# Block 2's gate stretch of a two-MLP kernel: transfers asked for four steps ahead in a held queue, the last norm's mean three steps later

## The chip, the cores and the metric

One core of a Trainium2 chip runs the whole program. The metric is the device time of one execution in microseconds (us); lower is better. The core's engines run their own instruction queues side by side and wait for each other by semaphores: TensorE (PE, matrix products; PEld is its weight load), VectorE (DVE), ScalarE (ACT), GpSimd (POOL) and SyncE (SP, whose queue here asks for nearly all transfers).

## The reference

Three stages, for 1536 tokens of width 512 (2 sequences of 768, 8 heads of 64). The weights of both MLPs and the scale of the norm are taken in double precision.

```python
state = gamma[None, :, None, None] * state + np.einsum('bhd,bhe->bhde', k[:, :, t], v[:, :, t])
y[:, :, t] = scale * np.einsum('bhd,bhde->bhe', q[:, :, t], state)
...
h = x @ w_in
g = h * (1.0 / (1.0 + np.exp(-1.702 * h)))
return (g @ w_out).astype(np.float32)
...
rms = np.sqrt(np.mean(x * x, axis=-1, keepdims=True) + 1e-06)
xn = x / rms * rms_g
g = xn @ w_gate
silu = g * (1.0 / (1.0 + np.exp(-g)))
val = xn @ w_val
return (silu * val @ w_out).astype(np.float32)
```

The first MLP is 512 to 2048 to 512, the second 512 to 1536 (gate and value) to 512.

## The kernel before

**Numbers.** Each float32 operand of a product is split into a high part (ScalarE's copy, name ending in h) and a low part (VectorE's difference, ending in l); `product` (L379) makes three matmuls of it: high by high (L383), high by low and low by high (L384, L385). A weight that comes in double precision (a tile `w_64`, `w<-in_w` in the rows) is converted by `convert` (L151): two copies on ScalarE (L163, L164), three steps on VectorE (L167, L168, L174), and for the second MLP's weights a store to DRAM (L180, `w27d<-qw`), to be read back by `reload` (L188, `w24r<-w24d`). `load_next` asks for the next double tile, `convert_next` converts one and calls `load_next`. In the trace all buffers of a pool go by one name: `w` is a double tile as well as a part of w3 (the second MLP's out-weights).

**Stages.** The 1536 tokens are three blocks of 512 columns. Attention runs for all; the first MLP has 16 slices f of 128 hidden units. Block 0 is computed in the loop over f with weights `wo`. Blocks 1 and 2 come from the chains m0 to m7 of `seven` (L692), which compute two slices for two blocks with seven products instead of eight (the steps use the operand combinations x, y, z; their banks are called a and b, the intermediate results p, q, r). Of each result, block 1's gate is used at once (`use_m`, L646: silu on ScalarE at L653, `gate_parts` at L421 and L422 splits it into gh and gl, out-weights `wowp`), and block 2's gate gm is stored to DRAM (`to_dram`). After the chains comes the **gate stretch** of block 2: for each f the gate gwm is read back, split, and multiplied by out-weights `wowq` into the banks acc. In it the norm of the earlier blocks runs on ScalarE and VectorE, and at its end the first sums of the second MLP's weights.

**The norm.** `norm_tasks` (L453) gives six tasks: two of squares sq and their sum with its split into sh and sl; the mean (two matmuls with `mean_w`, L479) with the first guess r and u (L483, L486); the `roots`; and two of scaling. There is one norm for each block; the last, of block 2, runs in the walk over the second MLP's first chains.

**The second MLP** has for each pair of slices (g = 0, 2, ...) two chains, g0, v0 and so on (gate and value), whose 14 steps are walked in turn; `work[n]` holds what is issued behind step n: the products o of earlier slices, conversions, reloads, the sums and splits of the next weights (`set_tasks`, L590: sums swg and swv at L611; operands wg2x, wg2y, wg2z and likewise wv), the norm's tasks, and `y_tasks`, the operands yo of block 2 (differences at L578, splits at L388). From the third pair on, the chains lg and lv of block 2 are walked behind each pair.

**What sets the order.** Every engine works its queue in order. A scheduler sets the order within an engine from the order in which the program is written and the times at which it takes buffers and operands to be ready; `after` (L123) adds a fixed order between two instructions, `in_order` (L104) one for all instructions of a stretch. A tile of a pool can be written only when the tile that had its buffer is no longer read, so a load waits for that. Pools here: `wr` 16 buffers, `tmp` 12, `wo` 3, `gs` 3, `st` 4. `wait_m` (L986) asks for gate and out-weights of f; it is called two steps ahead.

Of the kernel before, what the change touches and what calls it, by code (L numbers as in the profile page):

```python
# [8 lines left out]
F32 = mybir.dt.float32  # L9
# [27 lines left out]
FIRST, OTHER, LAST = 0, 1, 2  # L37
LAG = 3
JOIN = 4
HELD = 2  # L40
# [6 lines left out]
def tile_retention_mlp_swiglu(  # L47
# [56 lines left out]

    def in_order(first):

        last = {}
        for i in nc.cur_bb.bb.instructions[first:]:
            if i.engine in ENGINES:
                if i.engine in last:  # L110
                    after(i, last[i.engine])
                last[i.engine] = i
        return last
# [24 lines left out]

    def convert_next(split=False):
        n = count["converted"]  # L140
        if n < len(queue):
            rest = convert(*queue[n])
            count["converted"] += 1
            if split:
                return rest
            for step in rest:
                step()
            load_next()

# [58 lines left out]

    def load_wo(f, user):
        t = wo_p.tile([128, 1024], F32R, tag="wo", name=f"wo{user}{f}")  # L210
        parts[user, f] = both(t)
        nc.sync.dma_start(out=t.bitcast(F32), in_=kept["wo", f])
# [243 lines left out]
    def norm_tasks(j, p):  # L456
# [19 lines left out]
        def means():  # L476
            st["m"] = psum(p, f"mean{j}")
            for n, t in enumerate(st.pop("two")):
                nc.tensor.matmul(out=st["m"], lhsT=mean_w, rhs=t, start=n == 0, stop=n == 1)  # L479

        def guess():
# [167 lines left out]
    def use_m(p):  # L649
        def use(i, j, src, own):  # L650
            f = 2 * p + i
            if j == 0:
                nc.scalar.activation(out=own, in_=src, func=ACTF.Silu, scale=GELU)  # L653
                gate_parts(("wp", f), own)
                load_wo(f, "wp")
                fill.extend((f, m) for m in range(KD))
            else:
                t = later["gs"].tile([128, T], F32, tag="gs", name=f"gm{f}")
                nc.scalar.activation(out=t, in_=src, func=ACTF.Silu, scale=GELU)
                to_dram("m", f, t)  # L660
        return use
# [282 lines left out]
    assert not att  # L944

    lanes = [[(p, n) for p in range(k, F1 // 2, 2) for n in range(7)] for k in range(2)]
    chains = {
# [16 lines left out]
    for e, (p, n) in enumerate(order):  # L964
# [14 lines left out]
        if e > 12 and e % 2:  # L979
            if count["converted"] < 2 * F1 + 20:  # L980
                convert_next()
        if e in (24, 32):
            some(norm, 1)
    some(norm, 1)

    def wait_m(f):  # L986
        if f < F1:
            t = waiting["m", f] = later["gs"].tile([128, T], F32, tag="gs", name=f"gwm{f}")
            nc.sync.dma_start(out=t, in_=kept_g["m", f])
            load_wo(f, "wq")  # L990

# [9 lines left out]
    some(norm, 1)  # L1001
    wait_m(0)
    wait_m(1)
    gate_m(0)
    tasks = None
    for f in range(F1):
        wait_m(f + 2)
        gate_m(f + 1)
        some(norm, 2 if f == 0 else 1)
        if f == 0:  # L1010
# [3 lines left out]
        if f in (4, 5, 6, 8, 10, 12):  # L1014
            some(norm, 1)
        if f == 8:
            for x in range(2):
                reload("w2", x)
        if f == 10:
# [5 lines left out]
        if f == F1 - 1:  # L1025
            some(norm, len(norm))
            for n in (0, 3, 4):
                for t in sets:
                    t[n]()
        mlp1_out("wq", 2, f)  # L1030
    for m in range(KD):
        evacuate(2, m)
# [37 lines left out]
    for g in range(0, F2, 2):  # L1070
# [15 lines left out]
        if g == 0:  # L1086
            for n, t in zip((2, 4, 8, 11), norm):
                work[n].append(t)
        if g == 2:
            norm = norm[4:] + y_tasks()  # L1090
            for n, t in enumerate(norm):
                work[min(n, 13)].append(t)
# [117 lines left out]
```

## Time and profile before

| | |
|---|---|
| time, median of 3 runs | 592.88 us (592.82 to 595.37) |
| the profiled execution | 591.96 us, of which the span is 588.5 us |
| TensorE | 579.9 us busy (99%), 3264 matmuls |
| VectorE | 453.4 us busy (77%) |
| ScalarE | 363.1 us busy (62%) |
| GpSimd | 26.3 us busy (4%) |
| TensorE clock granted | 1.00 of full speed over the span |
| transfers | 135.09 MB, 230 GB/s |

The span runs from the first to the last instruction that the profiler records; the rest of the execution's time lies around it. The gate stretch lies at 260 to 309 us. A matmul's row shows 0.39 us, but the next one can start before it ends, so the space between two starts tells what one costs. TensorE's busy share hides small waits for the same reason; a wait shows as a wider space between two starts, and in the rows as the idle time in square brackets with what ended it.

### The profile page before, as it was taken

How to read it: one execution, taken by the hardware profiler on the slowest of the kernel's cores; microseconds unless marked ns; L12 is line 12 of the kernel's file. 1: busy time of each engine (PE TensorE's matmuls, PEld its weight loads, DVE VectorE, ACT ScalarE, POOL GpSimd, SP SyncE). 2: the span in 40 equal slices, each digit the busy share in tenths (PEclk: the TensorE clock that was granted, in tenths of full speed). 3: DMA queues.
4: the chain of work that ended last, by engine and by line, in shares of the span. 5: the costliest groups of instructions: out<-in, count | busy, mean ns of one | idle time of the engine just before them, and what ended most of it. 6: DMA issues, size and time to landing. Idle time of an engine off the chain costs nothing.

```text
span 588.5 us, 9253 instructions
## 1 busy us (share of the span) xinstructions
PE 579.9 (99%) x3264; PEld 480.7 (82%) x3264; DVE 453.4 (77%) x808; ACT 363.1 (62%) x688; POOL 26.3 (4%) x27
## 2 busy tenths in 40 slices
PE   8999999999999999999999999999999999999997
PEld 5787887888788888877877888888989889988885
DVE  2999897978999786649989999997765676654542
ACT  2686767766777786657457876555654445544432
POOL 4400321000000000000000000000000000000000
PEclk9999999999999999999999999999999999999999
DMA  8979989896379888888893555736323476543521
GB/s 323 400 241 404 356 301 360 288 308 249 142 240 340 296 273 311 285 302 294 301 336 121 184 150 173 235 107 215 108 71 108 122 264 227 175 144 121 167 72 71
DMA packets 47854, 135.09 MB, mean 230 GB/s; under 512 B 5568, under 2 KB 5824, under 8 KB 47808
## 3 DMA queue, kind: packets, MB, share of 16 engines
q1 hardware_dynamic: 47376, 134.37, 66.4%
q8 instruction: 25, 0.41, 0.3%
q10 hardware_dynamic: 432, 0.14, 0.1%
q14 instruction: 21, 0.17, 0.1%
HBM read 98.84 MB, written 35.65 MB: 229 GB/s over the span
## 4 chain that ended last, share of the span: by engine, by line
PE 83%; DMA 7%; DVE 5%; ACT 2%; issue 1%; SPq 0%; DVEq 0%
PE acc L383 6%; PE acc L385 6%; PE acc L384 6%; PE o L383 6%; PE o L384 6%; PE o L385 6%; PE h L406 5%; DMA w<-in_w 3%; DMA qk<-in_qk 1%; PE y L308 1%; DMA wowq<-wo11d 1%; PE m0a L711 1%; PE g4a L711 1%; DMA wm2d<-w 1%; PE sc L266 1%
## 5 line engine op out<-in xcount | busy, mean ns | idle before, releaser
L383 PE MATMUL o<-w,gh 128*128 128x512 f32 x144 | 56.2, 390 | 0.0
L384 PE MATMUL o<-w,gh 128*128 128x512 f32 x144 | 56.2, 390 | 0.0
L385 PE MATMUL o<-w,gl 128*128 128x512 f32 x144 | 56.1, 389 | 0.0
L168 DVE CUSTOM_DVE_ANT_0 qw<-qw,uw 128x1024 uint16<-128x1024 uint16 x68 | 47.3, 698 | 3.1 <-ACT uw L164 0.9
L163 ACT ACTIVATE qw<-w 128x512 f32<-128x512 f32 x68 | 45.1, 663 | 1.5 <-DMA w<-in_w 1.5
L164 ACT ACTIVATE uw<-w 128x512 uint32<-128x512 uint32 x68 | 45.3, 667 | 0.0
L167 DVE TENSOR_SCALAR qw<-qw 128x512 uint32<-128x512 uint32 x68 | 30.6, 451 | 17.2 <-ACT qw L163 17.2
L389 DVE TENSOR_TENSOR gl<-gw,gh 128x512 fp32r<-128x512 f32 x24 | 16.6, 692 | 26.1 <-ACT gh L388 26.0
L388 ACT ACTIVATE gh<-gw 128x512 fp32r<-128x512 f32 x24 | 15.1, 630 | 28.6 <-PE o L384 23.5
L385 PEld LDWEIGHTS o<-w,gl 128*128 128x128 f32 x144 | 27.0, 188 | 5.6
L384 PEld LDWEIGHTS o<-w,gh 128*128 128x128 f32 x144 | 27.1, 188 | 4.7
L383 PEld LDWEIGHTS o<-w,gh 128*128 128x128 f32 x144 | 27.1, 188 | 4.5
L383 PE MATMUL acc<-gh,wo 128*128 128x512 f32 x64 | 25.8, 411 | 0.0
L383 PE MATMUL acc<-gh,wowq 128*128 128x512 f32 x64 | 25.3, 396 | 0.5 <-DMA wowq<-wo11d 0.4
L385 PE MATMUL acc<-gh,wo 128*128 128x512 f32 x64 | 25.1, 393 | 0.0
L384 PE MATMUL acc<-gl,wo 128*128 128x512 f32 x64 | 25.1, 392 | 0.0
L384 PE MATMUL acc<-gl,wowp 128*128 128x512 f32 x64 | 25.1, 392 | 0.0
L384 PE MATMUL acc<-gl,wowq 128*128 128x512 f32 x64 | 25.0, 390 | 0.0
L385 PE MATMUL acc<-gh,wowp 128*128 128x512 f32 x64 | 24.9, 390 | 0.0
L385 PE MATMUL acc<-gh,wowq 128*128 128x512 f32 x64 | 24.9, 390 | 0.0
L174 DVE SCALAR_TENSOR_TENSOR qw<-w,qw 128x512 uint32<-128x512 uint32 x36 | 24.6, 685 | 0.2
L406 PE MATMUL h<-xt0h,wih 128*128 128x512 f32 x64 | 24.4, 397 | 0.2 <-ACT xt0h L329 0.2
(1512 smaller groups left out, 1693.4 us busy)
## 6 DMA issues: line engine op xcount, KB each, us to landing
w<-in_w SPq DMA_DIRECT2D x68, 512.0 KB, 5.9
qk<-in_qk SPq DMA_DIRECT2D x12, 512.0 KB, 7.9
kv<-in_kv SPq DMA_DIRECT2D x12, 512.0 KB, 8.3
gmd<-gm SPq DMA_DIRECT2D x16, 256.0 KB, 4.6
gwm<-gmd SPq DMA_DIRECT2D x16, 256.0 KB, 3.9
g1d<-gs SPq DMA_DIRECT2D x12, 256.0 KB, 2.5
g2d<-gl SPq DMA_DIRECT2D x12, 256.0 KB, 2.0
gw<-g1d SPq DMA_DIRECT2D x12, 256.0 KB, 2.7
```

Source lines behind the costliest of these rows:

```text
L163: nc.scalar.activation(out=q, in_=high.bitcast(F32), func=ACTF.Copy, scale=2.0 ** -112)
L164: nc.scalar.activation(out=t, in_=low, func=ACTF.Copy, scale=2.0 ** -29)
L167: lambda: nc.vector.tensor_scalar(out=m, in0=m, scalar1=3, scalar2=None, op0=ALU.logical_shift_left),
L168: lambda: nc.vector.tensor_tensor(out=m, in0=m, in1=t, op=ALU.add),
L174: nc.vector.scalar_tensor_tensor(out=dst, in0=high, scalar=0x80000000, in1=m, op0=ALU.bitwise_and, op1=ALU.bitwise_or)
L383: nc.tensor.matmul(out=out, lhsT=ah, rhs=bh, start=first, stop=False)
L384: nc.tensor.matmul(out=out, lhsT=ah, rhs=bl, start=False, stop=False)
L385: nc.tensor.matmul(out=out, lhsT=al, rhs=bh, start=False, stop=last)
L388: nc.scalar.activation(out=hi, in_=src, func=ACTF.Copy)
L389: nc.vector.tensor_tensor(out=lo, in0=src, in1=hi.bitcast(F32), op=ALU.subtract)
L406: nc.tensor.matmul(out=ps, lhsT=w[a][:, k * 128:(k + 1) * 128], rhs=x[b][:, k, :], start=o == order[0], stop=o == order[-1])
L711: nc.tensor.matmul(out=bank, lhsT=u, rhs=v, start=first and k == 0 and x == 0, stop=k == 1 and x == 2, skip_group_check=True,)
```

## The change

Five things, all in the order and the buffers; no arithmetic changes.

- `wait_m` becomes `load_wq`. The gate tile gwm comes from `tmp` (12) instead of `gs` (3), and out-weights of ten of the sixteen f from `wr` (16) instead of `wo` (3). It is called four steps ahead instead of two; the first four and the out-weights wowp15 are asked for inside the loop over the chains, at its fourth-last step.
- From there to the end of the gate stretch the transfers in SyncE's queue are held in the order of the program (`in_order`, now with a choice of engines).
- Four loads of double tiles (of w27 and w33), which the last conversions of the chain loop asked for, are asked for in steps 11 to 14 of the gate stretch; the two reloads of w2 go from step 8 to steps 6 and 8.
- A mean matmul is held behind the TensorE instruction that the program wrote last before it.
- The last norm's mean and guess go from step 8 to step 11 of the walk over g0 and v0, and its roots from step 11 to the next pair.

```diff
+AHEAD = 4
+WITH_WR = (0, 1, 2, 3, 4, 5, 6, 10, 11, 12)
...
-    def in_order(first):
+    def in_order(first, engines=ENGINES):
...
-            if i.engine in ENGINES:
+            if i.engine in engines:
...
-    def convert_next(split=False):
+    def convert_next(split=False, load=True):
...
-            load_next()
+            if load:
+                load_next()
...
-    def load_wo(f, user):
-        t = wo_p.tile([128, 1024], F32R, tag="wo", name=f"wo{user}{f}")
+    def load_wo(f, user, p=None):
+        p = p or wo_p
+        t = p.tile([128, 1024], F32R, tag=p.name, name=f"wo{user}{f}")
...
         def means():
             st["m"] = psum(p, f"mean{j}")
+            done = [i for i in nc.cur_bb.bb.instructions if i.engine == mybir.EngineType.PE][-1]
             for n, t in enumerate(st.pop("two")):
                 nc.tensor.matmul(out=st["m"], lhsT=mean_w, rhs=t, start=n == 0, stop=n == 1)
+                after(nc.cur_bb.bb.instructions[-1], done)
...
-                load_wo(f, "wp")
+                if ("wp", f) not in parts:
+                    load_wo(f, "wp")
...
+    def load_wq(f):
+        if f < F1:
+            t = waiting["m", f] = tmp(f"gwm{f}")
+            nc.sync.dma_start(out=t, in_=kept_g["m", f])
+            load_wo(f, "wq", wr_p if f in WITH_WR else wo_p)
...
-                convert_next()
+                convert_next(load=count["converted"] < 2 * F1 + 16)
         if e in (24, 32):
             some(norm, 1)
+        if e == len(order) - 4:
+            loads = len(nc.cur_bb.bb.instructions)
+            load_wo(F1 - 1, "wp")
+            for f in range(AHEAD):
+                load_wq(f)
...
-    def wait_m(f):
-        if f < F1:
-            t = waiting["m", f] = later["gs"].tile([128, T], F32, tag="gs", name=f"gwm{f}")
-            nc.sync.dma_start(out=t, in_=kept_g["m", f])
-            load_wo(f, "wq")
...
-    wait_m(0)
-    wait_m(1)
     gate_m(0)
     tasks = None
     for f in range(F1):
-        wait_m(f + 2)
+        load_wq(f + AHEAD)
         gate_m(f + 1)
+        if f > F1 - 6 and f < F1 - 1:
+            load_next()
...
-        if f == 8:
-            for x in range(2):
-                reload("w2", x)
+        if f in (6, 8):
+            reload("w2", f // 2 - 3)
...
         mlp1_out("wq", 2, f)
+    in_order(loads, [mybir.EngineType.SP])
...
         if g == 0:
-            for n, t in zip((2, 4, 8, 11), norm):
+            for n, t in zip((2, 4, 11), norm):
                 work[n].append(t)
         if g == 2:
-            norm = norm[4:] + y_tasks()
+            norm = norm[3:] + y_tasks()
```

The scheduler moves more than these lines. Three places follow, each as the engine's queue stands before and after. Lines of the kernel after are higher by 4 to 7 (L711 is now L718).

**At the end of the last chain.** TensorE, before: behind the last row of the chain's result m7b (bank b of m7) stand eight rows of slice 14 of block 1 (gate parts gl_2846 and gh_2845) and both rows of the mean of an earlier block, ahead of the products of slice 15, whose gate (gh_2910) is made from m7b.

```order
L711 MATMUL m7b<-xm_1920,wm7zl 128x512
L384 MATMUL acc_1_1875<-gl_2846,wowp_2849 128x512
L385 MATMUL acc_1_1875<-gh_2845,wowp_2849 128x512
L383 MATMUL acc_2_1876<-gh_2845,wowp_2849 128x512
L384 MATMUL acc_2_1876<-gl_2846,wowp_2849 128x512
L385 MATMUL acc_2_1876<-gh_2845,wowp_2849 128x512
L383 MATMUL acc_3_1877<-gh_2845,wowp_2849 128x512
L384 MATMUL acc_3_1877<-gl_2846,wowp_2849 128x512
L385 MATMUL acc_3_1877<-gh_2845,wowp_2849 128x512
L479 MATMUL mean_2928<-sh_2451,mean_w 128x512
L479 MATMUL mean_2928<-sl_2452,mean_w 128x512
L383 MATMUL acc_0_1874<-gh_2910,wowp_2914 128x512
```

TensorE, after, from the same row of m7b (slice 15's gate is gh_2920 here):

```order
L718 MATMUL m7b<-xm_1920,wm7zl 128x512
L484 MATMUL mean_2936<-sl_2452,mean_w 128x512
L387 MATMUL acc_0_1874<-gh_2920,wowp_2871 128x512
L387 MATMUL acc_1_1875<-gh_2920,wowp_2871 128x512
L387 MATMUL acc_2_1876<-gh_2920,wowp_2871 128x512
```

Of the ten rows one is left there; the others stand further up. ScalarE, after, at the same place (the silu is qm<-qm; before, r and u stood behind both gh):

```order
L666 ACTIVATE gm_2908<-m7a 128x512
L489 ACTIVATE r_2939<-mean_2936 128x512
L659 ACTIVATE qm_2829<-qm_2829 128x512
L492 ACTIVATE u_2940<-r_2939 128x512
L425 ACTIVATE gh_2920<-qm_2829 128x512
L425 ACTIVATE gh_2967<-gwm_2873 128x512
```

The norm's u now stands between the silu and the split of slice 15's gate.

**Where the last norm's mean stood.** TensorE, before, in the walk over g0 and v0 (o is a product of the second MLP's out-weights):

```order
L711 MATMUL g0a<-xh_3243,wg0yl 128x512
L479 MATMUL mean_3546<-sh_3489,mean_w 128x512
L383 MATMUL o_3708<-w_3712,gh_3457 128x512
L384 MATMUL o_3708<-w_3712,gh_3457 128x512
L385 MATMUL o_3708<-w_3712,gl_3458 128x512
L479 MATMUL mean_3546<-sl_3490,mean_w 128x512
L711 MATMUL v0a<-xh_3243,wv0yh 128x512
```

TensorE, after, from the same row of g0a:

```order
L718 MATMUL g0a<-xh_3243,wg0yl 128x512
L718 MATMUL v0a<-xh_3243,wv0yh 128x512
L718 MATMUL v0a<-xl_3244,wv0yh 128x512
L718 MATMUL v0a<-xh_3243,wv0yl 128x512
L718 MATMUL v0a<-xh_3243,wv0yh 128x512
```

The y products of v0a follow g0a's at once; the mean and the o products stand further down.

**At the first products of the second MLP.** VectorE, before, ahead of the addition pg<-g0b that ends the first product pair (w_3712 is a part of w30, swg and swv are sums of the weights w22 and w23):

```order
L447 COPY x_2_3394<-acc_3_2986 128x512
L611 TENSOR_TENSOR swg_3511<-swg_3511,w22r 128x256
L611 TENSOR_TENSOR swv_3520<-swv_3520,w22r 128x256
L611 TENSOR_TENSOR swg_3511<-w22r,w23r 128x256
L611 TENSOR_TENSOR swg_3511<-w22r,swg_3511 128x256
L611 TENSOR_TENSOR swv_3520<-w22r,w23r 128x256
L611 TENSOR_TENSOR swv_3520<-w22r,swv_3520 128x256
L389 TENSOR_TENSOR wg2zl<-w23r,wg2zh 128x256
L389 TENSOR_TENSOR wg2zl<-swg_3511,wg2zh 128x512
L721 TENSOR_TENSOR pg_3408<-g0b,pg_3408 128x512
```

VectorE, after, up to the same addition and past it:

```order
L451 COPY x_2_3394<-acc_1_2984 128x512
L451 COPY x_2_3394<-acc_3_2986 128x512
L393 TENSOR_TENSOR w_3710<-w30r,w_3710 128x512
L728 TENSOR_TENSOR pg_3408<-g0b,pg_3408 128x512
L170 TENSOR_SCALAR qw_3423<-qw_3423 128x512
L171 ISA qw_3423<-qw_3423,uw_3424 128x1024
```

The sums of w22 and w23 and the low parts of wg2z stand behind pg now, in the rows up to the first difference x<-x of block 2's operands. In TensorE's queue nine o products stood ahead of the first z product of g2a before; after, four do:

```order
L718 MATMUL v2a<-xh_3243,wv2yl 128x512
L387 MATMUL o_3706<-w_3815,gh_3617 128x512
L387 MATMUL o_3707<-w_3815,gh_3617 128x512
L387 MATMUL o_3708<-w_3815,gh_3617 128x512
L387 MATMUL o_3709<-w_3815,gh_3617 128x512
L718 MATMUL g2a<-xh_3269,wg2zh 128x512
```

The other o products of that slice come later.

## Rows read from the trace of the kernel before

**Rows 1.** Windows: length, busy PE, PEld, DVE, ACT, POOL, PEclk, DMA share, GB/s.

```profile
259.94:309.00 49.06, 48.50 (x209) 38.60 (x209) 45.60 (x69) 31.28 (x51) 0.00 (x0) 1.00 0.88 306
309.00:330.00 21.00, 19.59 (x86) 15.87 (x86) 20.66 (x42) 17.41 (x33) 0.00 (x0) 1.00 0.45 136
330.00:355.00 25.00, 25.00 (x112) 20.67 (x112) 25.00 (x45) 18.05 (x34) 0.00 (x0) 1.00 0.57 178
...
366.00:584.00 218.00, 218.00 (x1196) 189.75 (x1195) 140.99 (x274) 108.05 (x218) 0.00 (x0) 1.00 0.45 147
```

**Rows 2.** Timeline at m7's end: start, duration, engine, line, instruction, [idle before <-releaser].

```profile
257.44 0.39 PE L711 MATMUL m7b<-xm,wm7zl 128*128 128x512 f32 x1
...
257.87 0.69 DVE L721 TENSOR_TENSOR qm<-m7b,qm 128x512 f32<-128x512 f32 x1 [2.40 <-PE m7b L711]
...
258.60 0.63 ACT L653 ACTIVATE qm<-qm 128x512 f32<-128x512 f32 x1 [1.51 <-DVE qm L721]
...
259.94 0.96 PE L383 MATMUL acc<-gh,wowp 128*128 128x512 f32 x3
...
261.86 0.63 ACT L486 ACTIVATE u<-r 128x512 f32<-128x512 f32 x1
```

**Rows 3.** Timeline of TensorE in the gate stretch.

```profile
294.28 0.39 PE L711 MATMUL g0a<-xoh,wg0xh 128*128 128x512 f32 x1
295.07 0.50 PE L383 MATMUL acc<-gh,wowq 128*128 128x512 f32 x1 [0.41 <-DMA wowq<-wo11d]
...
308.61 0.39 PE L385 MATMUL acc<-gh,wowq 128*128 128x512 f32 x1
```

**Rows 4.** Timeline at the last norm's mean.

```profile
320.62 0.39 PE L711 MATMUL g0a<-xh,wg0yl 128*128 128x512 f32 x1
...
321.74 0.63 ACT L388 ACTIVATE sh<-sq 128x512 fp32r<-128x512 f32 x1 [0.29 <-DVE sq L470]
...
322.28 0.58 ACT L718 ACTIVATE qv<-v0a 128x512 f32<-128x512 f32 x1
...
322.42 0.50 PE L479 MATMUL mean<-sh,mean_w 128*128 128x512 f32 x1 [1.41 <-ACT sh L388]
```

**Rows 5.** Timeline of VectorE ahead of pg.

```profile
310.06 0.42 DVE L611 TENSOR_TENSOR swv<-swv,w22r 128x256 f32<-128x256 f32 x1
...
312.08 0.68 DVE L389 TENSOR_TENSOR wg2zl<-swg,wg2zh 128x512 fp32r<-128x512 f32 x1
```

**Rows 6.** Timelines of VectorE, ScalarE and TensorE around g2a's z products.

```profile
343.76 0.68 DVE L578 TENSOR_TENSOR x<-x 128x512 f32<-128x512 f32 x1
344.36 0.68 DVE L174 SCALAR_TENSOR_TENSOR qw<-w,qw 128x512 uint32<-128x512 uint32 x1
...
344.62 0.62 ACT L388 ACTIVATE yox<-x 128x512 fp32r<-128x512 f32 x1
...
347.30 0.59 ACT L718 ACTIVATE rg<-g2a 128x512 f32<-128x512 f32 x1
...
347.06 0.39 PE L384 MATMUL o<-w,gh 128*128 128x512 f32 x1
...
348.19 0.39 PE L711 MATMUL g2a<-xh,wg2zh 128*128 128x512 f32 x1
```

**Rows 7.** Timelines of VectorE and TensorE ahead of g4a's y products.

```profile
359.27 0.69 DVE L678 TENSOR_TENSOR qg<-qv,qg 128x512 f32<-128x512 f32 x1
...
360.78 0.39 PE L711 MATMUL v4b<-xol,wv4xl 128*128 128x512 f32 x1
```

**Rows 8.** SyncE's queue and a user on ScalarE; last, the page's DMA issues.

```profile
305.58 0.32 SPq L190 DMA_DIRECT2D w24r<-w24d  x1
...
321.13 0.32 SPq L180 DMA_DIRECT2D w27d<-qw  x1
...
335.57 0.61 ACT L388 ACTIVATE wg4xh<-w24r 128x512 fp32r<-128x512 f32 x1
...
w<-in_w SPq DMA_DIRECT2D x68, 512.0 KB, 5.9
```

## The prediction

> **What bounds the kernel now.** I read the page first: TensorE is busy for 99% of the span, so the question is only which waits of TensorE go and which come. Then the windows [rows 1]. From 259.94 to 309 us, the gate stretch of block 2, VectorE is busy for 45.60 of 49.06 us and ScalarE for 31.28. From 309 to 355 VectorE is full: 20.66 of 21.00 and 25.00 of 25.00, with ScalarE near 0.8 and 0.7. From 366 to 584 TensorE has 218.00 of 218.00 and VectorE 140.99. So there are three regimes: a gate stretch with small gaps, a stretch where VectorE has no room, and a long tail in which TensorE alone counts and a delay is handed on to the end. Last the timelines around the waits [rows 2 to 7]: matmul starts there are 0.226 us apart when nothing waits ((348.19 - 347.06) / 5) [rows 6], which is the pitch I use, since matmul ends overlap. On VectorE instructions stand 0.337 us apart when 256 wide (six from 310.06 to 312.08) [rows 5] and 0.60 when 512 wide (343.76 to 344.36); on ScalarE 0.54 (five from yox at 344.62 to rg at 347.30) [rows 6]. These are my slots.
>
> **Gaps removed in the gate stretch: -2.0.** The first product of wowp15 starts at 259.94, the last of wowq15 at 308.61 [rows 2, 3]: 48.67 us for 207 matmuls, which at the pitch need 206 x 0.2266 = 46.68. So 1.99 us is all that earlier transfers could give back here. The largest piece is wowq11's transfer: the product behind it starts 295.07 - 294.28 = 0.79 after the one ahead, a pitch and 0.56 us. With the load four steps ahead and most tiles from the pool of 16, that one has an answer: it goes. The rest are short waits for gl, the copies of acc, and the mean. Bounds: -0.6 (that transfer alone) and -2.0; I take -2.0, since every cause in the stretch is named by the change or by its new order.
>
> **The end of chain m7: +2.6.** After the last m7b matmul (257.44) the chain is qm on VectorE (257.87), silu on ScalarE (258.60), gh behind it, first product of wowp15 (259.94): 2.50 us [rows 2]. Before, ten matmuls stand behind m7b and cover it: eight of wowp14 and two of the mean; 2.50 is eleven pitches and TensorE waits for nothing. In the new order nine of the ten stand ahead of m7's last rows, and only the mean's second matmul is left behind m7b. The rows that moved cost nothing, but the cover is gone: 2.50 - 2 x 0.227 = 2.05. Besides, ScalarE's order becomes r, silu, u, gh, where r and u belong to the norm and stood behind gh before (u at 261.86). Now u stands inside the chain: +0.54, a slot. Sum 2.6. Bounds: 2.05 (u hidden) and 3.2 (r late as well). Term one and this one almost cancel: a cover was spent to close the gaps.
>
> **The mean moved from step 8 to 11: +0.4.** Before, the first mean matmul starts at 322.42, where the pitch after 320.62 would give 320.85: 1.57 of wait on sh, which waits for sq on VectorE [rows 4]; with the row behind it, 1.68. The edit removes that wait. What is late next: the row that now follows g0a is v0a's y product, which may be written only when ScalarE has copied v0a out (qv). On ScalarE qv stands directly behind sh, before and after. Before, qv starts at 322.28, so it lets TensorE go at 322.28 + 0.68 (sh at 321.74 to the mean at 322.42) = 322.96. Wait: 322.96 - 320.85 = 2.1 in place of 1.68. So the waiting instruction is exchanged, not the wait: queued behind it on TensorE is all of v0a and g0a. Bounds: -1.7 (sh lands ahead of v0a's row) and +1.0.
>
> **VectorE's order around g2a: +2.5.** Reading the new order against the old between the product pg<-g0b and the first difference x<-x of the y operands, twelve instructions come in, five go out. In: the eight sums swg/swv of w22r and w23r, both wg2zl, which before had been run when pg came, the last at 312.08 [rows 5]; wv4xl; and one conversion's third step. That is 9 x 0.337 + 3 x 0.60 = 4.83. Out: five sums, 1.69. VectorE has no idle time there to take 3.14 [rows 1], so x<-x starts at 343.76 + 3.14 = 346.9 at the earliest. Behind it on ScalarE stand yox (0.86 later), qw, uw, yoxt1l and the copy rg, which starts 0.86 + 4 x 0.54 = 3.0 later: 349.9 [rows 6]. TensorE's g2a z products need rg: 349.9 + 0.68 = 350.6. TensorE gets there earlier than before, since four o products stand ahead where nine stood: 348.19 - 5 x 0.226 = 347.06, plus the 1.0 of the terms so far = 348.1. Wait: 2.5. Bounds: 0 (x starts by 344.4) and 3.0 (x at 347.4, when pg's later start is handed on in full).
>
> **The copy pg of g4a: +0.5.** In ScalarE's new order it stands behind yo0l and gh, and this gh waits for VectorE's product qg, which before came at 359.27 [rows 7]. VectorE is behind by its 3.14 and by 0.5 of pg's later start: 362.9; gh 0.73 later (as 257.87 to 258.60 in rows 2), the copy a slot behind at 364.2, TensorE 0.68 behind that: 364.8. TensorE's row there follows the one at 360.78, which is now 360.78 + 3.5 = 364.3. Wait: 0.5. Bounds 0 and 1.5.
>
> **Late weights and the held queue: 0.** Four conversions' loads move from ahead of the gate stretch to behind wowq15's, and the queue of transfers is held in program order. A store that waits for VectorE then stands ahead of the loads queued behind it: w24r was asked for at 305.58, and in the new order it stands behind the second store of w27, at 321.13 before, and up to 3 later with VectorE: 324. A load of that size takes 5.9 us, so it lands by 330, and its first user, the split of wg4's x, is at 335.57 [rows 8]. So I take 0, covered by some 5 us; bounds 0 and +3. The four moved loads themselves now stand right behind wowq15's, whose first product starts twelve rows before the end of the stretch, at 306; they need to be there only for conversions that stand behind g0a's products, past 312. The order put on the mean matmuls is between rows of TensorE itself, gwm in another pool and w2's two reloads at two steps are no new rows: nothing for these, and GpSimd has no changed row.
>
> **Sum.** -2.0 + 2.6 + 0.4 + 2.5 + 0.5 = +4.0 on the profiled 591.96 us: 596.0. The median of the runs lies 0.92 above that execution: **596.9**. From 366 on TensorE has no idle share in which this could go [rows 1].
>
> **A rule weighed.** The rows show a gap of 0.56 us on TensorE that a transfer ended [rows 3], and VectorE at 25.00 of 25.00 later [rows 1]. The Trainium skill, Perfetto Trace Analysis, section Optimization Strategy, tells the reader to find the gaps on the most contended engine and to make what they wait for start sooner; by that the change would win the gaps' 3.7 us (the first rival below). The same section says that in some kernels the most contended engine changes over time, and this trace agrees: VectorE's full windows follow the gate stretch, and work pushed there would come back as waits.
>
> **Rivals.**
> *Gaps close, nothing new (faster).* The gate stretch gives 2.0, the mean's wait 1.7, and the chain at m7 and rg stay covered: 592.88 - 3.7 = 589.2. For it: each wait named is really there. Against it: the new order has one row of cover behind m7b where ten stood. It decides at m7b's end: no idle there. Chance 0.08.
> *VectorE catches up (no measurable change).* If VectorE comes to pg so much earlier, with the sums gone from ahead of it, that the 3.14 are run in time that it idles now, x<-x starts by 344.4, rg's copy ends by 348.1 and both later waits vanish: 592.88 - 2.0 + 2.6 + 0.4 = 593.9. For it: VectorE idles for 3.46 of the 49.06 us before 309. Against it: it executes in order, and pg, behind which the sums now stand, waits for TensorE's g0b. It decides at x<-x. Chance 0.22.
> *Transfers come too late (slower).* w24r's load, behind the store, lands after wg4 x needs it: up to 3 more, 599.9. For it: the queue is held. Against it: the 5 us of cover worked out above. Chance 0.08.
> *Forecast*, 596.9 with its own range 595.3 to 598.5: 0.62.
>
> **How the numbers follow.** 0.5%, about what a measurement of this kernel can tell from no change, is 2.96 us: 589.9 to 595.8. Of the forecast's 0.62, about 0.08 lies below 595.8, since the forecast is only 1.1 above the bound and a smaller wait for rg would do it. Slower: 0.54 + 0.08 = 0.62; same: 0.08 + 0.22 = 0.30; faster 0.08. The range takes in the no-change rival and the late transfers and leaves the faster rival out: 593.7 to 599.8.
>
> **What will show it.** Right: no wait on wowq's transfer; TensorE idle for about 2.6 us after m7b's last row, ended by gh; no mean where it was, but about 2 us of idle ahead of v0a's y product, ended by qv; about 2.5 ahead of g2a's z product, ended by rg, with VectorE full before it; half a microsecond ahead of g4a's y product, ended by pg. Wrong: no idle behind m7b (then the whole reading of the new order falls, and the change gains); x<-x starting no later than before against TensorE's rows; or waits on w24r or w27 that I costed at nothing.

## The result, and the profile after

| | before | after |
|---|---|---|
| time, median of 7 runs | 592.82 us (591.82 to 595.37) | 597.52 us (595.09 to 598.04) |
| the profiled execution | 591.96 us, span 588.5 us | 597.10 us, span 595.0 us |
| forecast | | 596.9 us (593.7 to 599.8) |

The ratio is 1.0072, with a 95% interval of 1.0050 to 1.0093: the change makes the kernel 3.0 to 5.5 us slower. TensorE's list of waits from 259 us to the end has three entries after. Each line names what waits and what it waits for, then us in total, times, and the longest; the list gives the idle time of the row, some 0.16 us less than the start-to-start space without the pitch, which the text calls the wait.

```profile
PE g2a L718 <- ACT rg L725: 2.5, 1, 2.5
PE acc L387 <- ACT gh L425: 2.3, 1, 2.3
PE v0a L718 <- ACT qv L725: 1.9, 1, 1.9
```

and had two before, the mean's 1.4 on sh and the 0.4 of the transfer of wowq11, for which rows 3 and 4 stand. All three new ones are ended by ScalarE. The timeline of the kernel after at the end of chain m7, to be laid beside [rows 2]:

```profile
260.13 0.39 PE L718 MATMUL m7b<-xm,wm7zl 128*128 128x512 f32 x1
260.35 0.39 PE L484 MATMUL mean<-sl,mean_w 128*128 128x512 f32 x1
260.55 0.69 DVE L728 TENSOR_TENSOR qm<-m7b,qm 128x512 f32<-128x512 f32 x1 [4.34 <-PE m7b L718]
260.78 0.60 ACT L489 ACTIVATE r<-mean 128x512 uint32<-128x512 uint32 x1 [0.99 <-PE mean L484]
261.28 0.63 ACT L659 ACTIVATE qm<-qm 128x512 f32<-128x512 f32 x1
261.81 0.61 ACT L492 ACTIVATE u<-r 128x512 f32<-128x512 f32 x1
262.33 0.61 ACT L425 ACTIVATE gh<-qm 128x512 fp32r<-128x512 f32 x1
...
263.00 1.19 PE L387 MATMUL acc<-gh,wowp 128*128 128x512 f32 x4 [2.26 <-ACT gh L425]
```

One matmul stands where ten did, u stands between the silu and gh, and from the mean's start to the first product of wowp15 there are 2.65 us: a pitch (0.227 us, the space between two starts where nothing waits) and 2.42 of wait. From that product to the last of wowq15 the gate stretch now runs without a gap (the row of the last one, then the window):

```profile
309.60 0.39 PE L389 MATMUL acc<-gh,wowq 128*128 128x512 f32 x1
```
```profile
263.00:310.00 47.00, 47.00 (x207) 38.95 (x208) 43.00 (x65) 28.24 (x46) 0.00 (x0) 1.00 0.82 294
```

From one to the other there are 206 matmuls now, one less than before, since the mean's first one is among those that moved. They take 46.60 us from first start to last, and 205 pitches are 46.45. Where the mean stood ([rows 4]), v0a's product waits for the copy behind sh:

```profile
321.84 0.39 PE L718 MATMUL g0a<-xh,wg0yl 128*128 128x512 f32 x1
...
322.95 0.63 ACT L392 ACTIVATE sh<-sq 128x512 fp32r<-128x512 f32 x1 [1.91 <-DVE sq L474]
...
323.49 0.58 ACT L725 ACTIVATE qv<-v0a 128x512 f32<-128x512 f32 x1
...
324.12 0.50 PE L718 MATMUL v0a<-xh,wv0yh 128*128 128x512 f32 x1 [1.89 <-ACT qv L725]
```

And at g2a ([rows 6]) x<-x comes at 348.17 instead of 343.76, and rg with it. First VectorE's pg<-g0b, before and after, then the kernel after (VectorE, ScalarE, TensorE):

```profile
312.89 0.69 DVE L721 TENSOR_TENSOR pg<-g0b,pg 128x512 f32<-128x512 f32 x1
```
```profile
314.11 0.69 DVE L728 TENSOR_TENSOR pg<-g0b,pg 128x512 f32<-128x512 f32 x1 [0.88 <-PE g0b L718]
...
348.17 0.69 DVE L584 TENSOR_TENSOR x<-x 128x512 f32<-128x512 f32 x1
...
348.89 0.63 ACT L392 ACTIVATE yox<-x 128x512 fp32r<-128x512 f32 x1 [3.92 <-DVE x L584]
...
351.05 0.58 ACT L725 ACTIVATE rg<-g2a 128x512 f32<-128x512 f32 x1
...
348.15 1.07 PE L387 MATMUL o<-w,gh 128*128 128x512 f32 x4
351.69 0.80 PE L718 MATMUL g2a<-xh,wg2zh 128*128 128x512 f32 x1 [2.47 <-ACT rg L725]
352.29 0.63 PE L718 MATMUL g2a<-xl,wg2zh 128*128 128x512 f32 x1
352.71 0.63 PE L718 MATMUL g2a<-xh,wg2zl 128*128 128x512 f32 x1
...
354.42 0.53 PE L718 MATMUL v2a<-xh,wv2zh 128*128 128x512 f32 x1
354.79 0.39 PE L718 MATMUL v2a<-xl,wv2zh 128*128 128x512 f32 x1
```

From pg to x<-x VectorE needs 34.06 us where it needed 30.87: 3.19 more, for 61 rows between them in place of 54. Behind the wait the matmuls stand 0.426 us apart, not 0.227, and the windows (length, busy PE, PEld, DVE, ACT, POOL, then PEclk, DMA share, GB/s) say why:

```profile
330.00:348.50 18.50, 18.50 (x83) 15.20 (x82) 18.39 (x33) 12.47 (x23) 0.00 (x0) 1.00 0.38 119
348.50:351.60 3.10, 0.72 (x4) 0.26 (x2) 3.10 (x8) 2.71 (x6) 0.00 (x0) 0.95 0.85 235
351.60:354.60 3.00, 2.91 (x7) 2.33 (x8) 3.00 (x7) 1.56 (x4) 0.00 (x0) 0.50 0.78 291
```

TensorE was full up to 348.5 and then waited for most of 3 us; the granted clock fell to 0.50, the lower of its two levels (1.2 GHz, the upper being 2.4), for the next 3 us. From 351.69 to 354.79 seven matmuls take 3.10 us, 1.51 more than at full clock. VectorE is busy for 18.39 of 18.50 us and then without a break: it is the engine that sets when x<-x comes.

The time between the two profiled executions, term by term (each measured as the start-to-start space less the pitches in it, after less before):

| term | forecast | measured |
|---|---|---|
| gaps in the gate stretch | -2.0 | 0.15 - 1.99 = -1.84 |
| end of chain m7 | +2.6 | +2.42 |
| mean's wait, then v0a's | +0.4 | 2.05 - 1.68 = +0.37 |
| g2a's z product | +2.5 | 3.54 - 4 x 0.227 = +2.63 |
| g4a's y product | +0.5 | 0 in this execution |
| half clock behind g2a's wait | not foreseen | +1.51 |
| sum | +4.0 | +5.09 |

The two executions differ by 5.14. That the sums agree so well is partly luck: TensorE's last matmul starts 6.04 later (584.44 and 590.48), of which 0.65 had come about by the end of m7, ahead of the first changed wait (2.69 at m7b's last row, less the nine rows that moved ahead of it), 0.3 belongs to no term, and 0.9 is given back in what lies behind that matmul and around the span (7.52 and 6.62 us).

### The profile page after: what moved, and what is told of

It reads as the page before. It is cut to its first block, busy times and chain, and to the rows that moved or that the text cites. A ratio compares the mean times of both kernels' runs of the same rounds, so it can differ in the third digit from the quotient of the medians.

```text
span 595.0 us, 9255 instructions
## 1 busy us (share of the span) xinstructions
PE 581.9 (98%) x3264; PEld 483.4 (81%) x3264; DVE 454.7 (76%) x808; ACT 362.5 (61%) x688; POOL 26.4 (4%) x27
## 4 chain that ended last, share of the span: by engine, by line
PE 87%; DVE 6%; ACT 3%; issue 2%; DMA 2%; DVEq 0%; ACTq 0%
PE acc L387 7%; PE acc L389 7%; PE acc L388 7%; PE o L388 5%; PE o L389 5%; PE o L387 5%; PE h L410 5%; PE sc L270 2%; PE y L312 2%; PE y L299 1%; DMA w<-in_w 1%; DVE w L177 1%; DVE qw L171 1%; PE m0a L718 1%; PE g10a L718 1%
## 5 line engine op out<-in xcount | busy, mean ns | idle before, releaser
L170 DVE TENSOR_SCALAR qw<-qw 128x512 uint32<-128x512 uint32 x68 | 32.0, 470 | 16.3 <-ACT qw L166 16.3
L387 PE MATMUL acc<-gh,wowp 128*128 128x512 f32 x64 | 24.0, 391 | 2.3 <-ACT gh L425 2.3
L389 PE MATMUL acc<-gh,wowp 128*128 128x512 f32 x64 | 24.9, 389 | 0.0
```

The lines of the kernel that those rows point to most:

```text
L170: lambda: nc.vector.tensor_scalar(out=m, in0=m, scalar1=3, scalar2=None, op0=ALU.logical_shift_left),
L387: nc.tensor.matmul(out=out, lhsT=ah, rhs=bh, start=first, stop=False)
L389: nc.tensor.matmul(out=out, lhsT=al, rhs=bh, start=False, stop=last)
```

## The experiments

The kernel before, run beside them, had medians of 592.31, 591.67 and 591.93 us in the three groups below (runs 1 to 4, 5 to 8, 9 to 11); each ratio is against the one of its group. Most intervals are 1 to 2 us wide on either side, so a part of the change that is worth less shows in the waits of the profile and not in the ratio. The prediction read the new order off the queues and did not say which of the five parts of the change made it. The theory tried here: the loads four steps ahead close gaps in the gate stretch, and the order that the scheduler makes of the held queue and the late loads spends two covers, at m7b and at g2a. A cover is the rows that an engine can work through while a chain of dependent instructions on other engines is still under way.

**1. Cover put back by hand.** In the kernel after, slice 14's twelve products are held behind m7b.

```diff
+        ended = [i for i in nc.cur_bb.bb.instructions if i.engine == mybir.EngineType.PE][-1]
+        begun = len(nc.cur_bb.bb.instructions)
         while len(fill) > 4:
             f, m = fill.popleft()
             mlp1_item("wp", 1, f, m)
+        if e == len(order) - 1:
+            for i in nc.cur_bb.bb.instructions[begun:]:
+                if i.engine == mybir.EngineType.PE:
+                    after(i, ended)
```

> The kernel after, with the twelve products of slice 14 held behind the last row of m7b in TensorE's queue, so that fourteen rows stand there again instead of one. Theory (a spent cover): the 2.4 us wait of the first wowp15 product goes, nothing takes its place, the waits at v0a (2.05), at g2a (2.6) and the slow clock behind it stay: 597.5 - 2.4 = 595.1 us. Rival 1 (the chain is late for another reason, the wait goes to the next product that needs gl or gwm): 597.5 to 597.0. Rival 2 (the twelve rows covered something ahead of m7a's last rows): up to 2.7 of new wait there, 597.8.

596.40 us, 1.0062 (1.0043 to 1.0082); by the ratios 0.6 us less than after, where 2.4 was expected, though the two intervals together leave room for anything from 1.1 more to 2.3 less. TensorE's waits in its profile:

```profile
PE v0a L718 <- ACT qv L725: 2.4, 1, 2.4
PE g2a L718 <- ACT rg L725: 2.3, 1, 2.3
PE m7a L718 <- ACT rm L725: 0.7, 1, 0.7
PE g4a L718 <- ACT pg L725: 0.4, 1, 0.4
```

The wait for gh is gone, so the cover was its cause. But a part of rival 2 is true: the twelve products had stood ahead of m7a's last rows and covered a copy there (0.7). The wait at v0a grows by 0.5, and one of 0.4 appears at g4a. The clock stays at 1.00 behind g2a in this profile, so its slow stretch did not stay in every execution. A cover taken from one place is missed at the next.

**2. qv ahead of sh.** In the kernel after, the last norm's split may not start before ScalarE has copied v0a.

```diff
         def two_sums():
             st["two"] = [tmp(f"s{n}{j}").bitcast(F32R) for n in "hl"]
+            begun = len(nc.cur_bb.bb.instructions)
             halves(*st["two"], st.pop("s"))
+            if "qv0" in copied:
+                after(nc.cur_bb.bb.instructions[begun], copied["qv0"])
...
-            for n, t in zip((2, 4, 11), norm):
+            for n, t in zip((2, 6, 11), norm):
```

(`copied` holds the copy instructions of `seven` by name.)

> The kernel after, with ScalarE's copy qv of v0a ordered ahead of sh (the last norm's squares and split are issued two steps later), so that v0a's y product need not wait. VectorE's queue from pg<-g0b to x<-x keeps its 61 rows. Theory (VectorE is full from pg to x<-x and sets when rg comes): the wait of 2.05 at v0a goes and comes back in full at g2a, 2.6 becomes about 4.7, the time stays at 597.5 within 0.6. Rival (the waits add up independently): the 2.05 is won, 595.5, and g2a still waits 2.6.

600.28 us, 1.0132 (1.0115 to 1.0149): neither. The wait left v0a, but it came back before g2a (one of 0.4 at g4a is left out here):

```profile
PE g0a L722 <- ACT rg L729: 3.2, 1, 3.2
PE acc L387 <- ACT gh L425: 2.3, 1, 2.3
PE g2a L722 <- ACT rg L729: 1.8, 1, 1.8
```

ScalarE's timeline in this kernel shows why. qv is early (320.07), and the next copy that TensorE needs, rg of g0a, stands behind sh and two conversions:

```profile
320.07 0.60 ACT L729 ACTIVATE qv<-v0a 128x512 f32<-128x512 f32 x1
...
323.48 0.63 ACT L392 ACTIVATE wg2yh<-swg 128x512 fp32r<-128x512 f32 x1 [0.95 <-DVE swg L621]
324.96 0.63 ACT L392 ACTIVATE sh<-sq 128x512 fp32r<-128x512 f32 x1 [0.85 <-DVE sq L474]
...
327.14 0.59 ACT L729 ACTIVATE rg<-g0a 128x512 f32<-128x512 f32 x1
```

The waits of g0a, g2a and g4a, 3.2, 1.8 and 0.4, are together 1.0 more than v0a's and g2a's were, 1.9 and 2.5; what is saved at one comes back at the next. Most of the loss is half clock: granted 0.50 from 262.5 to 265.7, behind m7b's wait, where the kernel after had 1.00, and from 327.8 to 334 behind g0a's. At half of its length that costs 1.6 and 3.1 us, against 1.5 in the profile of after.

**3. The four weights loaded early again.**

```diff
-                convert_next(load=count["converted"] < 2 * F1 + 16)
+                convert_next()
...
-        if f > F1 - 6 and f < F1 - 1:
-            load_next()
```

> The kernel after, with the four loads of w27 and w33 asked for by the conversions again, as before. In VectorE's queue the sums of w22 and w23 then stand ahead of pg again (58 rows from pg to x<-x, not 61), with ten o products ahead of g2a's z product, not four; the mean of the earlier block stands wholly ahead of m7's last rows, so no row covers m7b. Theory (the late loads push w22's and w23's reloads, and with them the sums, behind pg): the wait at g2a and the slow clock behind it (2.6 + 1.5) go, m7b's wait stays at 2.3, v0a's at 2.0: 597.5 - 4.1 = 593.4 us. Rival (the wait at g2a comes from the norm's roots, moved to the next pair): g2a still waits 2.5, 597.4.

598.36 us, 1.0100 (1.0085 to 1.0115). The part on g2a is right: no wait there, though SyncE's queue is held in this kernel too. So the hold alone does not make that wait, and the norm's roots, which the rival named, do not make it either. The part on m7 is wrong: the wait for gh is 5.4, not 2.3, and half clock follows it for 5.7 us.

```profile
PE acc L387 <- ACT gh L425: 5.4, 1, 5.4
PE v0a L718 <- ACT qv L725: 1.9, 1, 1.9
```

In VectorE's queue of this kernel the norm's scaling stands ahead of qm, and in ScalarE's the split of its result ahead of the silu (two timelines, VectorE first):

```profile
261.64 1.42 DVE L503 SCALAR_TENSOR_TENSOR x<-r,g_sb,x 128x512 f32<-128x512 f32 x2
262.97 0.68 DVE L728 TENSOR_TENSOR qm<-m7b,qm 128x512 f32<-128x512 f32 x1
...
263.09 1.06 ACT L392 ACTIVATE xoh<-x 128x1024 fp32r<-128x1024 f32 x1 [1.91 <-DVE x L503]
264.05 0.61 ACT L659 ACTIVATE qm<-qm 128x512 f32<-128x512 f32 x1
```

I had read TensorE's queue for the cover and taken the chain's length from before. With the norm pulled ahead, qm starts at 262.97, 3.3 us behind m7b's last row (259.64) and not 0.4.

**4. The queue not held.**

```diff
-    in_order(loads, [mybir.EngineType.SP])
```

> The kernel after, with SyncE's queue not held. Eight products and both rows of the mean then stand behind m7b as before, and VectorE's sums stand ahead of pg as in the kernel with early loads. Theory (the held queue is what spent both covers, through the order that the scheduler makes of it): no wait at m7b, none at g2a, v0a waits 2.0; the transfers in their old freedom give 0 to 1 of waits in the gate stretch: 591.0 to 592.5. Rival (four steps ahead need the held order, or else out-weights come late): waits on wowq of 2 or more in the gate stretch, 593 to 596.

592.60 us, 1.0000 (0.9975 to 1.0024): without this one line the whole loss is gone, and nothing is won. TensorE's waits:

```profile
PE v0a L718 <- ACT qv L725: 1.9, 1, 1.9
PE mean L484 <- DVE sl L393: 0.5, 1, 0.5
```

m7b and g2a wait for nothing (0.1 us at g2a), and TensorE waits for no transfer, so the loads four steps ahead do not need the held order. Why nothing is won although the gate stretch lost 2 us before: v0a still waits for 2.0, and the time goes with the clock. Four of the ten executions had a mean granted clock of 0.999 or more and took 590.8 to 592.1 us; the six with 0.996 to 0.998 took 592.5 to 595.0. Behind which wait the clock fell in those six was not traced.

**5. Held only from the gate stretch on.**

```diff
-            loads = len(nc.cur_bb.bb.instructions)
...
     tasks = None
+    loads = len(nc.cur_bb.bb.instructions)
     for f in range(F1):
```

> The kernel after, with SyncE's queue held only from the loop of the gate stretch on, so that the first transfers, asked for inside the loop over the chains, are free. In TensorE's queue ten rows then stand behind m7b's last row as before; VectorE's queue from pg to x<-x stays as in the kernel after (61 rows). Theory (the hold has two separate prices, its part inside the chain loop costs m7b's cover, its part in the gate stretch the order of the sums): no wait at m7b, 2.0 at v0a, about 2.6 at g2a, up to 0.6 at g4a; 597.5 - 2.4 = 595.1, or 596 where g4a's wait comes up as it did with the cover restored by hand. Rival (the hold is one thing, and with it loosened at the start the wait at g2a changes too): 592 to 594.

594.98 us, 1.0041 (1.0017 to 1.0065). Waits: v0a 2.4, g2a 2.3, g4a 0.4, none at m7b. So the hold has two prices. Its first part, inside the loop over the chains, costs the cover of m7b (1.0072 - 1.0041, 1.8 us by the ratios, with intervals that just reach 0 together); the rest, together with the late loads (run 3), costs the order at g2a. The wait there is as long as it was, so the rival is out.

**6. The last norm's mean back in step 8.**

```diff
-            for n, t in zip((2, 4, 11), norm):
+            for n, t in zip((2, 4, 8, 11), norm):
...
-            norm = norm[3:] + y_tasks()
+            norm = norm[4:] + y_tasks()
```

> The kernel after, with the last norm's mean back in step 8 and its roots in step 11. Theory: the wait of 2.05 at v0a becomes the old one of 1.7 on sh at the mean; m7b's 2.4 stays; g2a's z products still wait, about 1.8, since four o products stand ahead and VectorE has one 512 wide row and the roots less between pg and x<-x; 597.5 - 0.4 - 0.8 = 596.3, and up to 1.5 less where the shorter wait leaves the clock at full speed. Rival (moving the mean is what made the wait at g2a): no wait there, 593.4.

596.34 us, 1.0075 (1.0047 to 1.0103). Waits: g2a 2.4, gh 2.3, the mean 1.4 again, g4a 0.5. The median is the one expected, but by the ratios nothing can be told from after: g2a waits 2.4 and not 1.8, and in the profile there is half clock behind both long waits, m7b's and g2a's. The rival is out: the moved mean did not make the wait at g2a.

**7. Only the mean moved**, in the kernel before (the same two lines, the other way).

> The kernel before, with only the last norm's mean in step 11 and its roots in the next pair. Theory: the wait of 1.68 at the mean becomes 2.05 at v0a's y product, released by qv; no wait at g2a, where fourteen o products stand ahead; 592.3 + 0.4 = 592.7. Rival (the move is worth what it seems to be, a wait of 1.7): 590.6.

592.71 us, 1.0011 (0.9991 to 1.0031): the rival's 1.7 us less is outside, the expected 0.4 more cannot be told from nothing, and the place is not the expected one. The mean's first matmul still stands directly behind g0a's row, though it was issued three steps later:

```profile
PE mean L479 <- ACT sh L388: 1.9, 1, 1.9
```

**9. The mean moved and held**, in the kernel before: the lines of run 7 and the change's own two lines in `means` (`done` and `after`).

> The kernel before, with the last norm's mean in step 11 as in the run that moved it alone, and with each mean matmul held behind the TensorE row that the program wrote ahead of it. v0a's y product now follows g0a's at once. Theory: the wait of 1.7 on sh at the mean becomes 2.05 at v0a's y product, released by qv; at g2a, where ten o products stand ahead and VectorE has 58 rows from pg, no wait or one under 0.5; 591.7 + 0.4 to 0.9 = 592.1 to 592.6. Rival (what the move takes away is won): 590.0, no wait at v0a.

593.92 us, 1.0028 (1.0003 to 1.0053). Now the mean is gone from there, and v0a waits:

```profile
PE v0a L713 <- ACT qv L720: 2.3, 1, 2.3
PE acc L383 <- ACT x L449: 1.7, 1, 1.7
```

So the third term is shown apart from the others: moving and holding the mean exchanges one wait for a longer one. The median is above the expected 592.6. This profile has two reasons for it: half clock behind v0a's wait (granted 0.50 from 324.9 to 328.1, some 1.6 us), and waits in the gate stretch that are 2.2 us longer together than before's. The largest of them is the second line above, a copy of acc that came late on ScalarE, as in run 10.

**8. Both copies ahead of the norm, queue free.** The kernel after without the hold (run 4), the norm's split ordered behind rg instead of qv, issued in step 9.

```diff
-    in_order(loads, [mybir.EngineType.SP])
...
+            if "rg0" in copied:
+                after(nc.cur_bb.bb.instructions[begun], copied["rg0"])
...
-            for n, t in zip((2, 4, 11), norm):
+            for n, t in zip((2, 9, 11), norm):
```

> The kernel after, with SyncE's queue not held, and the last norm's squares and split issued in step 9 with sh ordered behind ScalarE's copy rg of g0a, so that both copies, qv and rg, stand ahead of sh. VectorE has 53 rows from pg to x<-x, thirteen o products stand ahead of g2a's z product. Theory (what TensorE waits for at v0a is a copy queued behind the norm's split): no wait at v0a, at g0a's z or at g2a; against the kernel with the queue free 592.6 - 2.0 = 590.6 or less. Rival (as in the run with qv alone ahead, the wait goes on to the next copy or to the mean): 592.6 or more, with a wait of about 2 in another place.

590.25 us, 0.9968 (0.9952 to 0.9984): faster than both kernels. What TensorE still waits for:

```profile
PE mean L487 <- DVE sl L393: 0.7, 1, 0.7
PE g4a L722 <- ACT pg L729: 0.7, 1, 0.7
```

No copy is waited for at v0a, g0a's z or g2a, so the theory holds; some 0.7 comes back at g4a. Against run 4 the ratios give 1.9 us, and all ten executions have a mean granted clock of 0.998 or more.

**10. The same order in the kernel before**, without the loads and the rest of the change.

> The kernel before, with the last norm's squares and split issued in step 9, sh ordered behind ScalarE's copy rg of g0a, mean in step 11, roots in the next pair; loads and SyncE's queue as before. Theory: the wait of 1.7 goes and nothing takes its place at v0a, g0a's z or g2a; the gate stretch keeps its 2.0; 591.7 - 1.7 = 590.0. Rival (the gain of the run with rg first came from the loads four steps ahead): 591.7.

592.57 us, 1.0005 (0.9986 to 1.0024): the gain of run 8 is not there. The wait at the mean is gone, but waits on wowq11 (1.0), on a copy of acc (1.0), on sl (0.6) and at g4a (0.7) stand in the profile. The theory's 590.0 lies outside the interval. The rival's account, that run 8 won by its loads four steps ahead, fits the waits on transfers. The copy of acc is one of them too: in ScalarE's queue it stands behind a split of the gate tile that waits for its transfer.

```profile
264.27 0.63 ACT L421 ACTIVATE gh<-gwm 128x512 fp32r<-128x512 f32 x1 [1.48 <-DMA gwm<-gmd]
```

From m7b's last row to the last product of wowq TensorE loses 4.3 us beyond the pitches here, 1.6 in run 8 and 0.9 in run 4. Runs 7 and 9, which also load two steps ahead, lose 4.4 and 4.2; the profile of before, 2.0. Whether that comes from these kernels or changes from execution to execution is open, since each has one profile. But run 4 had the loads four steps ahead and won nothing either. By the ratios each part alone gives nothing (1.0000 and 1.0005), and both together give 0.9968, so it takes both.

**11. Run 8 with early weights and the cover of run 1.**

> The kernel with rg first, loads four steps ahead and SyncE's queue free (590.2), and in addition the four loads of w27 and w33 asked for early as before and slice 14's twelve products held behind m7b's last row. Theory: m7b was covered already, so the cover changes nothing, or costs the 0.85 ahead of m7a's rows that it cost in the kernel after; the early loads cost or win at most 0.5: 590 to 591. Rival (the late loads were a relief for the gate stretch's transfers, or a burden): 591.5 or more, or 589 or less, with waits on transfers in the gate stretch that come or go.

596.36 us, 1.0070 (1.0046 to 1.0094): worse by 6 than run 8. The cover costs 0.7 ahead of m7a's rows, as in run 1. Most of the loss is one wait, in the gate stretch, at the mean of the middle norm:

```profile
PE mean L487 <- ACT sh L392: 3.6, 1, 3.6
```

ScalarE waits there for the reload of w20, and what stands behind in its queue, the norm's squares and sh, comes late:

```profile
271.73 0.63 ACT L392 ACTIVATE wg0xh<-w20r 128x512 fp32r<-128x512 f32 x1 [5.29 <-DMA w20r<-w20d]
```

So the expected 590 to 591 is wrong, and the time is the rival's (591.5 or more), by a transfer that TensorE never waits for directly: it cost 3.6 through ScalarE's queue, with half clock behind it. Run 8 has the same split at 265.34, with 0.7 of idle time ahead of it. Which of the two edits made w20's reload late was not tried apart.

## Why the prediction was right

Forecast 596.9, measured 597.52; the first four terms are each within 0.2 us of the rows of the profile after.

- **Gate stretch, -2.0.** Right: 0.15 of 1.99 is left. No transfer is waited for.
- **m7, +2.6.** Right in size (2.42) and place, and in mechanism: with rows put behind m7b the wait goes (runs 1 and 5). The slot of u was counted with 0.54; it cost 0.39, since gh stood 0.66 behind the silu before and stands 1.05 behind it now.
- **Mean, +0.4.** Right: 0.37, released by qv behind sh as worked out, and shown alone in run 9. One thing I had not seen: neither the step number alone (run 7) nor the order held on the mean matmul alone (run 6) moves it; it takes both (run 9).
- **g2a, +2.5.** Right: 2.63. The added rows were worth 3.14 in the sum and 3.19 in the profile (pg to x<-x). Both ends of the wait lay a good microsecond later than worked out, x<-x at 348.17 against 346.9 (and beyond the bound of 347.4) and TensorE's arrival at g2a at 349.06 against 348.1, and this cancels: a part of the agreement is luck. In runs 3 and 4, where the sums stand ahead of pg again, the wait is gone, and for two reasons at once: pg to x<-x takes 32.7 there, 1.4 less, and ten o products stand ahead of g2a instead of four, six pitches or 1.4 more of cover.
- **g4a, +0.5.** 0 in the profile after, 0.6 in runs 1 and 5 (start to start). In the kernel after, the half clock behind g2a delays TensorE by 1.5, and the copy pg (365.81) is there 0.4 before TensorE needs it (366.83), which would account for it. Run 6 has both the half clock and 0.66 at g4a, but for a reason of its own: ScalarE waits for a reload just ahead of the copy. No run takes the half clock alone away, so the account stays argued.

```profile
365.05 0.42 ACT L392 ACTIVATE wg6zh<-w27r 128x256 fp32r<-128x256 f32 x1 [1.36 <-DMA w27r<-w27d]
```

- **Late weights and held queue, 0.** Right only in the narrow sense that TensorE waited for no transfer: w24r was asked for at 323.19, behind the second store of w27 as read, and its first user at 337.15 did not wait. The price of the held queue is in the order that the scheduler made of it, and that was counted under m7 and g2a. Run 4 shows that without the hold both go; run 3 shows that g2a's wait needs the late loads as well.
- **What was missing:** the lower clock behind a wait. A wait was priced at its length; the one at g2a cost 2.63 + 1.51. Among the seven runs of after, the one at 595.09 us had a mean granted clock of 0.999, the other six 0.993 to 0.998 and 597.1 us or more, so some 2 us of the median seem to hang on it. That the forecast came within 0.6 us is therefore luck in part: it lacked 1.5 of half clock, and against that it had 0.5 too much at g4a and 0.5 too much between the profiled execution and the median (0.92 counted, 0.42 measured).

**The rivals.** VectorE did not catch up: x<-x came 4.4 later, not 0.6. Gaps closing with nothing new was the other rival. Its gaps were really there, but here the order that came with closing them opened others. Run 4, without the hold, still waits at v0a and has the time of before; run 8, where that wait is gone too, wins 1.9 us by the ratio, half of the 3.7 that this rival expected. The late transfers' rival was out with w24r. (The stated range ends at 599.8, so it leaves out the last 0.1 of that rival, which it was said to take in.) The rule weighed with the rivals was from the Trainium skill, Perfetto Trace Analysis, section Optimization Strategy: find the gaps of the most contended engine, and make what they wait for start sooner. The traces agree that the gaps could be closed (1.99 in the gate stretch, 0.15 after); they show besides that this gains nothing while other waits open for it. The section's other sentence, that the most contended engine can change over time, agrees with these traces: VectorE is busy for 18.39 of the 18.50 us ahead of g2a's wait, where it sets the time, and for two thirds of the tail [rows 1].

## What to carry to other kernels

Before closing a gap, count the rows that stand behind the last instruction ahead of each dependent chain, and see whether the new order still has them: here one line that held a queue of transfers moved nine matmuls on TensorE and, with four loads asked for later, ten rows on VectorE. Read the queue of every engine in the chain, not just the one that waits, and what each row there waits for: the expectations of run 3 and run 11 failed by not doing so. Where a wait on a copy is removed, look at the next copy in the same queue, and order all of them ahead of the work that can wait, as run 8 does.

## What the runs showed of the hardware

The granted clock of TensorE fell to 0.50 behind some waits of 2.4 us and more (start to start, less the pitch) and not behind others. All such waits from m7's end on, in the profiles:

| kernel, place | wait | clock behind it |
|---|---|---|
| after, m7b | 2.42 | 1.00 |
| after, g2a | 2.63 | 0.50 for 3.0 us |
| run 1, v0a | 2.57 | 1.00 |
| run 1, g2a | 2.46 | 1.00 |
| run 2, m7b | 2.42 | 0.50 for 3.2 us |
| run 2, g0a | 3.35 | 0.50 for 6.2 us |
| run 3, m7b | 5.52 | 0.50 for 5.7 us |
| run 5, v0a | 2.56 | 1.00 |
| run 5, g2a | 2.47 | 1.00 |
| run 6, m7b | 2.42 | 1.00 for 0.5 us, then 0.50 for 3.4 |
| run 6, g2a | 2.53 | 0.50 for 3.0 us |
| run 9, v0a | 2.42 | 0.50 for 3.2 us |
| run 11, the middle norm's mean | 3.73 | 1.00 for 0.8 us, then 0.50 for 3.4 |

The same wait, at m7b with 2.42 us, was followed by full clock in one kernel and by half clock in two others, so its length alone does not decide. Shorter waits, of 2.1 us or less, were not followed by half clock in these profiles, but for one in run 11 that stood just behind a long one. The price is half of the time at half clock: 1.5 us after (g2a), 1.6 in run 9, and some 3 us in runs 2 (g0a) and 3. I had not expected a wait of under 3 us, in a stretch where TensorE is otherwise full, to cost more than itself. What sets whether it falls was not tried.
